# Local attention with a squared-Relu network behind it: in the last sequence, the scores of one and a half tiles in one stretch of the split TensorE array

## The chip, the cores and the metric

The kernel runs on one core of one Trainium2 chip. The metric is the device time of one execution in microseconds (us); lower is better. A core has TensorE (PE; its weight loads are shown as PEld), VectorE (DVE), ScalarE (ACT), GpSimd (POOL) and SyncE (SP), which work side by side and wait for each other by semaphores. Each takes its own instructions in the order in which the program gives them.

## The reference

Four sequences of 768 positions and 8 heads of 64. Each query sees the 96 latest positions and the first 8 positions of the sequence (the global keys), with a bias that falls with the distance; then a two-layer network with a squared Relu.

```python
scores = scale * np.matmul(q, k.transpose(0, 1, 3, 2))          # q, k, v: [4, 8, 768, 64]
keep = is_global | is_local                                      # pos < 8; 0 <= rel < 96
dist = np.where(is_global & ~is_local, float(n_local), np.abs(rel))
scores = np.where(keep, scores - slopes[:, None, None] * dist, -1e9)
a = softmax(scores)
x = np.matmul(a, v)                       # transposed and reshaped to [3072, 512]
g = np.maximum(x @ w_in, 0.0) ** 2        # w_in: [512, 2048]
out = g @ w_out                           # w_out: [2048, 512]
```

## The kernel before

**Tiles, blocks and steps.** The 3072 rows are 24 tiles `j` of 128 rows, six to a sequence, so tiles 18 to 23 are the last sequence. Two tiles make a block of the network, and a block is worked in 8 steps, each for 256 of the 2048 hidden columns: 12 blocks, steps 0 to 95. Step `n` has a first product (`s1`, L697: 8 matmuls of 128x256 into one PSUM bank `hT`), a Relu on ScalarE (`relu`, L718), a square on VectorE (`sq`, L730, out `hs`, 14 buffers) and a second product (`s2`, L767: 4 matmuls of 128x512 into the two banks `acc` of the block). `hr`, between Relu and square, has two buffers.

**Attention of a tile.** POOL loads `q`, `k` and `v` of the tile (L203), SyncE transposes queries and keys by DMA into `qkT` (L410; 12 buffers of it, SyncE's queue is in order). The scores (`sc`, L469) contract over 64 rows alone, so even and odd heads use the two halves of the array at the same time: a pair of matmuls, one in each half, each into its own bank. The first tile of a sequence has 8 such matmuls and two banks; every other tile looks at its own keys and at those of the tile to its left, in 16 matmuls and four banks (two groups `g` of four heads, each with two banks). One contiguous run of such matmuls is called a stretch. ScalarE takes the exponential of each bank (`exp`, L515), VectorE multiplies it with the exponential of the bias and mask (`mul`, L540), TensorE multiplies with the values (`pv`, L582, one bank for each of two halves of the heads), VectorE normalizes (`norm`, L609 and L610), and SyncE transposes the result by DMA into `xT` (L669), which the first product of the block needs.

**Global keys.** The global keys are the first 8 of a sequence. They are not kept apart: the mask leaves the first 8 columns of the left tile free for them. When the scores of tile `j` are done, `gk` (L556) overwrites the first 8 keys of tile `j` in `qkT` with the global ones, and the scores of tile `j+1` read them as those of its left tile. So the scores of `j+1` cannot come before the scores of `j` and the copy behind them. `gv` (L627) does the same for the values.

**Banks.** Two of the 8 PSUM banks are `acc`. The other six are one ring, `G`, in which transposes, scores, `hT` and `pv` take banks in the order in which the program opens them: a new bank waits for the users of the one six before it.

**Order.** The program's order is written by a planner, `Plan.run`, before anything is emitted. Every operation has its dependences, its cost on each engine, a key, and the ring it takes banks from; the planner goes through time, and picks the operation with the least sum of earliest start and 0.01 times its key. A result reaches another engine only after a lag. Keys make the first product run about four steps ahead of the second. For a tile the key comes from `base`, 8 times its block, less a lead (14 here), with 4 more for the second tile of a block. Besides, the scores of tile `j` may not come before the first product of step `4*j - 12`.

```python
            if n >= 0 and j >= NFIRST:
                o["deps"].append(s1_ops[n // NSTEP, n % NSTEP])
```

The kernel, as far as the diff touches it, with the line numbers of the profile:

Of the kernel before, what the change touches and what calls it, by code (L numbers as in the profile page):

```python
# [12 lines left out]
BF16 = mybir.dt.bfloat16  # L13
# [91 lines left out]
def kernel(  # L105
# [11 lines left out]
    nc = tc.nc  # L117
    B, H, S, D = q.shape
    P = 128
    d_model, d_ff = moe_w_in.shape  # L120
    assert D == 64 and S % 256 == 0 and H == 8 and d_model == H * D
    TPB = S // P
    NT = B * TPB
    NPAIR = H // 2
    KM = d_model // P
    KF = d_ff // P
    n_global = int(n_global)
# [8 lines left out]
    NSTEP = KF // 2  # L136
    NBLK = NT // 2
# [4 lines left out]
    NSPLIT = 4  # L142
    NBIAS = 3
    JQK, JX = 6, 8
    NQ, NKT = 3, 2 * TPB
# [9 lines left out]
    def const(shape, dt, name):  # L155
        return consts.tile(shape, dt, name=name, tag=name)
# [5 lines left out]
    qkT = [const([P, 2, NPAIR, P], BF16, f"qkT_{i}") for i in range(NKT)]  # L162
# [14 lines left out]
    plan = Plan()  # L177
    LEADS = {6: 10, 7: 11} | {j: 14 for j in range(10, NT)}
    SAFE = {j: 1.6 for j in range(6, 12)}
    SAFEX = {9: 1.5, 11: 1.5}  # L180
    JGATE = 11
    NHS = 14
    NWARM = 8
    NLATE, NO = 2, 4
    LEAD = 12
# [107 lines left out]
    for g in range(NFIRST + 2, NT, 6):  # L293
        js = range(g, min(g + 6, NT))
        o = plan.op(
            ("ones", g), {"DVE": 0.2}, lambda e, js=js: emit_ones(e, js),
            key=-1.0, ready=15.0,
        )
# [14 lines left out]
    def vec(cost):  # L313
        return {"DVE": cost}
# [20 lines left out]
    ]  # L335

    tiles = {}
    kT_users = [[] for _ in range(NKT)]
    qk_users = [[] for _ in qk_ring]
    xT_op = {}  # L340
# [5 lines left out]
    for j in range(NT):  # L346
        b, t = divmod(j, TPB)
        first = t == 0
        need = 8 * (j // 2)
        base = need - LEADS.get(j, LEAD) + 4 * (j % 2)  # L350


        if j in late:
# [3 lines left out]
            if NFIRST + 2 + NQ - 1 <= j < JGATE:  # L357

                def emit_gate(e, j=j):
# [4 lines left out]
                    key=base - 9,  # L364
# [3 lines left out]
                deps=qk_users[slot(j)] + [ones[j], gate], key=base, ready=issue[0],  # L368
# [7 lines left out]
        ku = kT_users[j % NKT]  # L376
        fp = j < NPLAIN
        parts = []
        for n in range(2) if j < JQK else ():
            users = []  # L380

            def emit_tr(e, j=j, n=n, fp=fp):
# [11 lines left out]
                deps=[land["qk"[n], j]], key=base, takes=(*G, [users]),  # L394
            )

            def emit_T(e, j=j, n=n, T_=T_):
                any_copy(e, T_[:, n], tiles.pop(("tr", n, j)))

            c = plan.op(  # L400
                ("T", n, j), {"DVE": 0.61 if fp else 0.41, "ACT": 0.48}, emit_T,
                deps=[tr] + ku, key=base + 0.1,
            )
# [4 lines left out]
        if j >= JQK:  # L408
            def emit_dT(e, j=j, T_=T_):
# [7 lines left out]
                deps=[land["q", j], land["k", j], xT_op[j - 3]] + ku, key=base - 6,  # L417
# [6 lines left out]
            parts = [T]  # L424
# [4 lines left out]
        groups = 1 if first else 2  # L429
# [32 lines left out]
                opened.add((odd, g))  # L462

        def emit_sc(e, gs, j=j, todo=todo, open_sc=open_sc):
            if j >= NBIAS:
                open_sc(gs)
            for g, pair, at, kt, odd in todo(gs):
                half = slice(odd * D, (odd + 1) * D)
                nc.tensor.matmul(  # L469
                    out=tiles["sc", j, odd, g][:, at, :],  # L470
                    lhsT=qkT[(j - kt) % NKT][half, 1, pair, :],
                    rhs=qkT[j % NKT][half, 0, pair, :],
                    start=j >= NBIAS,
                    stop=True,
                    skip_group_check=True,
                )

        deps = list(parts)
        if not first:
            deps += tiles["kready", j - 1] + [glob.get(("k", j - 1))]  # L480
        s_ = {}
        for gs in [(0,), (1,)] if j < NSPLIT and not first else [tuple(range(groups))]:
            n = 8 * len(gs)
            sc_users = busers[2 * gs[0] : 2 * gs[-1] + 2]
            takes = (*G, sc_users)
            bias = None
            if j < NBIAS:
                bias = plan.op(
                    ("bias", j, gs[0]), {"PE": 0.056 * n},
                    lambda e, gs=gs, f=emit_bias: f(e, gs), deps=[tr],  # L490
                    key=base + 0.9 + 2 * gs[0], takes=takes,
                )
                takes = None
            o = plan.op(
                ("sc", j, gs[0]), {"PE": 0.2 + 0.029 * n},
                lambda e, gs=gs, f=emit_sc: f(e, gs), deps=[*deps, bias],
                key=base + 1 + 2 * gs[0], takes=takes,
            )
            for us in sc_users:
                us.append(o)  # L500
            ku.append(o)
            if not first:
                kT_users[(j - 1) % NKT].append(o)
            s_.update({g: o for g in gs})
        for g in range(groups):
            for odd in range(2):
                users = busers[2 * g + odd]
# [41 lines left out]
                musers.append(m_)  # L549
                mul[odd, g], mul_users[odd, g] = m_, musers  # L550
        tiles["kready", j] = list(parts)


        if 1 <= t < TPB - 1:
            def emit_gk(e, j=j, t=t):
                nc.vector.tensor_copy(  # L556
                    qkT[j % NKT][:, 1, :, :n_global], qkT[(j - t) % NKT][:, 1, :, :n_global]
                )

            glob["k", j] = plan.op(  # L560
                ("gk", j), vec(0.1), emit_gk, deps=list(s_.values()), key=base + 4
            )
            kT_users[j % NKT].append(glob["k", j])
            kT_users[(j - t) % NKT].append(glob["k", j])
# [4 lines left out]
        for hf in range(2):  # L569
            users = []  # L570
# [167 lines left out]
    for o in plan.ops:  # L738
        if o["name"][0] == "sc":
            j = o["name"][1]  # L740
            n = 4 * j - LEAD
            if n >= 0 and j >= NFIRST:
                o["deps"].append(s1_ops[n // NSTEP, n % NSTEP])

    for blk in range(NBLK):
        last = blk == NBLK - 1
        acc_users = {}

        parts = [(0, None), (1, 0), (1, 1)] if last else [(0, None), (1, None)]
        order2 = (  # L750
            [(s, *p) for p in parts for s in range(NSTEP)]
            if last
            else [(s, *p) for s in range(NSTEP) for p in parts]
        )
        for s, sub, half in order2:
            users = acc_users.setdefault((sub, half), [])
            w = d_model if half is None else d_model // 2
            cols = slice(0, w) if half is None else slice(half * w, (half + 1) * w)
            own = half == 1

            def emit_s2(e, blk=blk, s=s, sub=sub, half=half, w=w, cols=cols, own=own):
                if s == 0:
                    pool, tag = (ps_g, "g") if own else (ps_acc, "acc")
                    tiles["acc", blk, sub, half] = pool.tile([P, w], FP32, name="acc", tag=tag)
                hs = tiles["hs", blk, s]
                for c in range(2):
                    nc.tensor.matmul(  # L767
                        out=tiles["acc", blk, sub, half],
                        lhsT=hs[:, c, sub * P : (sub + 1) * P],
                        rhs=w_out_sb[s][:, c, cols],  # L770
                        start=(s == 0 and c == 0),
                        stop=(s == NSTEP - 1 and c == 1),
                        skip_group_check=True,
                    )

            d, husers = square[blk, s]
            o = plan.op(
                ("s2", blk, s, sub), {"PE": 0.43 * w / d_model}, emit_s2,
                deps=[d, land["wout", s]] + users[-1:],
                key=8 * blk + s + 2.0 + (0 if not last else 8 * sub + 8 * (half or 0)),  # L780
                takes=((*G, [users]) if own else ("acc", NACC, [users])) if s == 0 else None,
            )
            users.append(o)
            husers.append(o)
            if s == NSTEP - 1:
                ousers = []

                def emit_o(e, blk=blk, sub=sub, half=half, cols=cols):
                    o_sb = work.tile([P, d_model], FP32, name="o", tag="o", bufs=NO)
                    any_copy(e, o_sb[:, cols], tiles["acc", blk, sub, half])  # L790
                    tiles["o", blk, sub, half] = o_sb

                ev = plan.op(
                    ("o", blk, sub), {"ACT": 0.48, "DVE": 0.61} if half is None else {"ACT": 0.28},
                    emit_o, deps=[o], key=8 * blk + s + 1.0, takes=("o", NO, [ousers]),
                )
                users.append(ev)
                ousers.append(ev)

                def emit_st(e, blk=blk, sub=sub, half=half, cols=cols):  # L800
                    r0 = (blk * 2 + sub) * P
                    nc.sync.dma_start(
                        out=out[r0 : r0 + P, cols],
                        in_=tiles.pop(("o", blk, sub, half))[:, cols],
                    )


                st = plan.op(
                    ("st", blk, sub), {"SP": 0.4}, emit_st,
                    deps=[ev, s1_ops[NLATE, 0] if blk < NLATE - 2 else None],  # L810
                    key=8 * blk + s + 9.0,
                )
                st = plan.op(("stored", blk, sub), {"DMAQ": 1.4}, None, deps=[st])
                ousers.append(st)
# [39 lines left out]
```

The softmax here doesn't subtract the row's maximum and nothing guards it: scores larger than these inputs give would overflow.

## Time and profile before

| | |
|---|---|
| time, median of 4 runs | 212.94 us (212.62 to 213.42) |
| the profiled execution | 212.88 us, of which its span 211.1 us |
| busy in the span | PE 203.5, PEld 142.3, DVE 142.2, ACT 117.6, POOL 73.9 us |
| granted clock of TensorE | 1.00 |
| first product, L697 | 768 matmuls, 98.3 us |
| second product, L767 | 369 matmuls recorded, 94.2 us |
| scores, L469 | 352 matmuls (192 of own keys, 160 of left keys) |
| in-place copies of global keys, L556 | 16 on VectorE, 215 ns each |

The span runs from the first to the last instruction, times in a timeline count from its start, and the rest of the execution's time lies around it. A line of a timeline gives start, length, engine, line of the kernel, operation, what it writes and reads, and how often; in brackets stands how long the engine was idle before, and for whom it waited. Matmuls are pipelined, so the lengths of neighbouring groups overlap, and the distance of their starts is the time that they take. Some matmul records are missing. The six stretches of the last sequence begin at 137.12, 144.74, 152.84, 160.93, 169.02 and 177.12 us.

### The profile page before, as it was taken

How to read it: one execution, taken by the hardware profiler on the slowest of the kernel's cores; microseconds unless marked ns; L12 is line 12 of the kernel's file. 1: busy time of each engine (PE TensorE's matmuls, PEld its weight loads, DVE VectorE, ACT ScalarE, POOL GpSimd, SP SyncE). 2: the span in 40 equal slices, each digit the busy share in tenths (PEclk: the TensorE clock that was granted, in tenths of full speed). 3: DMA queues.
4: the chain of work that ended last, by engine and by line, in shares of the span. 5: the costliest groups of instructions: out<-in, count | busy, mean ns of one | idle time of the engine just before them, and what ended most of it. 6: DMA issues, size and time to landing. Idle time of an engine off the chain costs nothing.

```text
span 211.1 us, 4968 instructions
## 1 busy us (share of the span) xinstructions
PE 203.5 (96%) x1953; PEld 142.3 (67%) x1984; DVE 142.2 (67%) x368; ACT 117.6 (56%) x221; POOL 73.9 (35%) x91
## 2 busy tenths in 40 slices
PE   7999999999999999999999999999999999999993
PEld 3777877656767766666676766666666766666772
DVE  7598878523877867876786786666786876644530
ACT  6797578114846755646456466456366465533531
POOL 8997765440675067140724505404000000000000
PEclk9999999999999999999999999999999999999999
DMA  8999999999999999959899997999443122120202
GB/s 124 154 170 187 183 191 199 176 215 130 178 146 151 174 135 168 224 70 153 85 199 143 137 198 97 138 171 133 86 106 75 45 82 28 25 99 3 99 0 101
DMA packets 112615, 27.32 MB, mean 129 GB/s; under 512 B 103248, under 2 KB 109648, under 8 KB 112592
## 3 DMA queue, kind: packets, MB, share of 16 engines
q0 software_dynamic: 79200, 13.37, 84.0%
q1 hardware_dynamic: 33392, 13.64, 32.2%
q8 instruction: 15, 0.25, 0.4%
q14 instruction: 8, 0.07, 0.1%
HBM read 27.26 MB, written 6.29 MB: 159 GB/s over the span
## 4 chain that ended last, share of the span: by engine, by line
PE 87%; POOL 5%; DMA 4%; issue 1%; ACT 1%; DVE 1%; POOLq 0%
PE hT L697 39%; PE acc L767 38%; PE sc L469 5%; PE po L582 4%; DMA win<-in_moe_w_in_dram 4%; POOL qk L203 3%; POOL v L203 2%; POOL win L203 1%; ACT hr L718 1%; PE tr L386 0%; PE trx L645 0%; DVE hs L730 0%; ACT esc L515 0%; ACT o L318 0%; DVE qkT L556 0%
## 5 line engine op out<-in xcount | busy, mean ns | idle before, releaser
L718 ACT ACTIVATE hr<-hT 128x512 f32<-128x512 f32 x96 | 58.1, 606 | 75.5 <-PE hT L697 73.3
L697 PE MATMUL hT<-xT,win 128*128 128x256 bf16 x768 | 98.3, 273 | 0.7 <-DMA win<-in_moe_w_in_dram 0.4
L767 PE MATMUL acc<-wout,hs 128*128 128x512 bf16 (+1 forms) x369 | 94.2, 370 | 2.0 <-issue 0.6
L697 PEld LDWEIGHTS <-win 128*128 128x128 bf16 x768 | 74.6, 98 | 26.7 <-DMA win<-in_moe_w_in_dram 0.7
L730 DVE TENSOR_TENSOR hs<-hr 128x512 bf16<-128x512 f32 x96 | 65.7, 688 | 34.2 <-ACT hr L718 33.9
L767 PEld LDWEIGHTS <-hs 128*128 128x128 bf16 x400 | 35.4, 98 | 22.1
L203 POOL DMA_DIRECT2D qk<-in_q_dram x23 | 20.8, 904 | 65.3 <-DMA qkT<-qk 49.6
L515 ACT ACTIVATE esc<-sc 128x512 bf16<-128x512 f32 x78 | 41.4, 612 | 1.2 <-PE sc L469 0.6
L540 DVE TENSOR_TENSOR at<-esc,E 128x512 bf16<-128x512 bf16 x78 | 31.9, 423 | 4.1 <-ACT esc L515 2.1
L203 POOL DMA_DIRECT2D v<-in_v_dram x24 | 21.9, 911 | 1.4 <-DMA win<-in_moe_w_in_dram 1.0
L610 DVE TENSOR_TENSOR x<-po,rs 128x256 bf16<-128x256 f32 x48 | 20.4, 425 | 1.7
L203 POOL DMA_DIRECT2D qk<-in_k_dram x23 | 20.7, 908 | 0.5 <-DMA win<-in_moe_w_in_dram 0.5
L582 PEld LDWEIGHTS <-at 128*128 128x128 bf16 x352 | 16.0, 98 | 6.2 <-issue 0.3
L582 PE MATMUL po<-v,at 128*128 128x65 bf16 x352 | 18.0, 193 | 0.3 <-DVE v L627 0.2
L318 ACT COPY o<-acc 128x512 f32<-128x512 f32 (+1 forms) x17 | 9.2, 563 | 8.1 <-PE acc L767 7.6
L469 PEld LDWEIGHTS <-qkT 64*128 64x128 bf16 x352 | 10.0, 94 | 5.5 <-issue 4.8
L469 PE MATMUL sc<-qkT 64*128 64x128 bf16 x192 | 13.2, 219 | 0.0
L609 DVE RECIPROCAL rs<-po 128x4 f32<-128x4 f32 x48 | 8.8, 184 | 6.1 <-PE po L582 5.4
L469 PE MATMUL sc<-qkT,qkT 64*128 64x128 bf16 x160 | 11.4, 216 | 0.0
L556 DVE COPY qkT<-qkT 128x32 bf16<-128x32 bf16 x16 | 3.4, 215 | 9.1 <-PE sc L469 9.0
L203 POOL DMA_DIRECT2D win<-in_moe_w_in_dram x8 | 6.2, 805 | 1.7 <-DMA win<-in_moe_w_in_dram 1.1
L320 DVE COPY o<-acc 128x512 f32<-128x512 f32 x8 | 5.5, 692 | 1.7 <-PE acc L767 1.6
(41 smaller groups left out, 64.6 us busy)
## 6 DMA issues: line engine op xcount, KB each, us to landing
out_dram<-o SPq DMA_DIRECT2D x23, 256.0 KB, 3.4
v<-in_v_dram POOLq DMA_DIRECT2D x24, 128.0 KB, 5.5
qk<-in_q_dram POOLq DMA_DIRECT2D x23, 128.0 KB, 5.0
qk<-in_k_dram POOLq DMA_DIRECT2D x23, 128.0 KB, 5.2
win<-in_moe_w_in_dram POOLq DMA_DIRECT2D x8, 256.0 KB, 8.0
wout<-in_moe_w_out_dram POOLq DMA_DIRECT2D x8, 256.0 KB, 9.2
qkT<-qk SPq DMA_TRANSPOSE x18, 5.4
plain<-in_q_dram SPq DMA_DIRECT2D x1, 256.0 KB, 3.3
```

The costliest lines, as they stand in the source:

```text
L203: nc.gpsimd.dma_start(out=dst, in_=src)
L318: nc.scalar.copy(dst, src)
L469: nc.tensor.matmul(out=tiles["sc", j, odd, g][:, at, :], lhsT=qkT[(j - kt) % NKT][half, 1, pair, :], rhs=qkT[j % NKT][half, 0, pair, :], s ...
L515: nc.scalar.activation(out=esc, in_=tiles.pop(("sc", j, odd, g)).rearrange("p a c -> p (a c)"), func=Act.Exp, scale=scale,)
L540: nc.vector.tensor_mul(at, tiles.pop(("esc", j, odd, g)), bias)
L582: nc.tensor.matmul(out=po[:, hi, :], lhsT=tiles["at", j, odd, g][:, at * P : (at + 1) * P], rhs=v_sb[kj][:, h, :], start=(i == 0), stop=(i ...
L609: nc.vector.reciprocal(rs, po[:, :, D : D + 1])
L610: nc.vector.tensor_tensor(out=x[:, 4 * hf : 4 * hf + 4, :], in0=po[:, :, :D], in1=rs.to_broadcast([P, 4, D]), op=Alu.mult,)
L697: nc.tensor.matmul(out=hT[:, c, :], lhsT=w_in_sb[s][:, kt, c * P : (c + 1) * P], rhs=tiles["xT", blk][:, kt, :], start=(kt == 0), stop=(kt ...
L718: nc.scalar.activation(hr, tiles.pop(("hT", blk, s)), Act.Relu)
L730: nc.vector.tensor_mul(hs, hr, hr)
L767: nc.tensor.matmul(out=tiles["acc", blk, sub, half], lhsT=hs[:, c, sub * P : (sub + 1) * P], rhs=w_out_sb[s][:, c, cols], start=(s == 0 an ...
```

## The change

The scores of tile 19 go into one operation, and so one stretch, with those of tile 18; the first half (group 0) of tile 21 with tile 20; tile 22 with the second half (group 1) of tile 21. Each of these takes all six banks of the ring. Tile 23 stays alone. The stretches are set right behind the first product of steps 60, 68, 74 and 80 (`STEP`), and the first product of the next step waits for them (`HOLD`). `base` of tiles 19, 21 and 22 is 4 less. So that the scores of 21 need not wait for the scores of 20, nor those of 22 for those of 21, the keys of tiles 20 and 21 are copied to a tile of their own (`kl`) when they have landed, with the global keys in the first 8 columns; the left-hand matmuls of 21 and 22 read them there, and `gk` of 20 and 21 is gone. `SETS` says for tiles 1 to 3 what the code said before; `BEHIND` is empty and does nothing.

```diff
+    SETS = {1: [(0,), (1,)], 2: [(0,), (1,)], 3: [(0,), (1,)], 21: [(0,), (1,)]}
+    JOIN = {(22, 0), (21, 0), (19, 0)}
+    COPY = [20, 21]
+    BEHIND = {}
+    HOLD = ((18, 0), (20, 0), (21, 1), (23, 0))
+    STEP = {(18, 0): 60, (20, 0): 68, (21, 1): 74, (23, 0): 80}
...
+    kl = [const([P, NPAIR, P], BF16, f"kl_{i}") for i in range(2 if COPY else 0)]
...
         base = need - LEADS.get(j, LEAD) + 4 * (j % 2)
+        if (j, 0) in JOIN:
+            base -= 4
...
         def emit_sc(e, gs, j=j, todo=todo, open_sc=open_sc):
+            if isinstance(gs, list):
+                for f, gs in gs:
+                    f(e, gs)
+                return
...
-                    lhsT=qkT[(j - kt) % NKT][half, 1, pair, :],
+                    lhsT=left[j - 1][half, pair, :] if kt else qkT[j % NKT][half, 1, pair, :],
...
-        for gs in [(0,), (1,)] if j < NSPLIT and not first else [tuple(range(groups))]:
+        for gs in SETS.get(j, [tuple(range(groups))]):
...
+            if (j, gs[0]) in JOIN:
+
+                o, also, taken = joint
+                also.append((emit_sc, gs))
+                taken += sc_users
+                o["deps"] += [d for d in deps if d is not None]
+                o["engines"]["PE"] += 0.029 * n
...
+        left[j] = qkT[j % NKT][:, 1]
+        if j in COPY:
+
+            left[j] = kl[COPY.index(j) % len(kl)]
+            users = left_users[j] = []
+
+            def emit_kl(e, j=j, t=t):
+                nc.vector.tensor_copy(left[j], qkT[j % NKT][:, 1])
+                nc.vector.tensor_copy(
+                    left[j][:, :, :n_global], qkT[(j - t) % NKT][:, 1, :, :n_global]
+                )
+
+            c = plan.op(
+                ("kl", j), vec(0.35), emit_kl, deps=parts, key=base - 3.5,
+                takes=("kl", len(kl), [users]),
+            )
...
-        if 1 <= t < TPB - 1:
+        if 1 <= t < TPB - 1 and j not in COPY:
             def emit_gk(e, j=j, t=t):
...
-            n = 4 * j - LEAD
+            n = STEP.get(o["name"][1:], 4 * j - LEAD)
             if n >= 0 and j >= NFIRST:
                 o["deps"].append(s1_ops[n // NSTEP, n % NSTEP])
+                if o["name"][1:] in HOLD:
+                    n += 1
+                    s1_ops[n // NSTEP, n % NSTEP]["deps"].append(o)
```

More of the change, by code (lines that the diff above doesn't have):

```diff
@@ L337 @@
     tiles = {}
+    left, left_users = {}, {}
+    kl = [const([P, NPAIR, P], BF16, f"kl_{i}") for i in range(2 if COPY else 0)]
     kT_users = [[] for _ in range(NKT)]
@@ L481 @@
         s_ = {}
-        for gs in [(0,), (1,)] if j < NSPLIT and not first else [tuple(range(groups))]:
+        for gs in SETS.get(j, [tuple(range(groups))]):
             n = 8 * len(gs)
             sc_users = busers[2 * gs[0] : 2 * gs[-1] + 2]
+            if (j, gs[0]) in JOIN:
[4 more added lines that the diff above has]
+                o["engines"]["PE"] += 0.029 * n
+                for us in sc_users:
+                    us.append(o)
+                ku.append(o)
+                if j - 1 in COPY:
+                    left_users[j - 1].append(o)
+                elif not first:
+                    kT_users[(j - 1) % NKT].append(o)
+                s_.update({g: o for g in gs})
+                continue
             takes = (*G, sc_users)
             bias = None
+            also = [(emit_sc, gs)]
             if j < NBIAS:
@@ L495 @@
                 ("sc", j, gs[0]), {"PE": 0.2 + 0.029 * n},
-                lambda e, gs=gs, f=emit_sc: f(e, gs), deps=[*deps, bias],
+                lambda e, gs=also, f=emit_sc: f(e, gs), deps=[*deps, bias],
                 key=base + 1 + 2 * gs[0], takes=takes,
             )
+            joint = o, also, sc_users
             for us in sc_users:
@@ L501 @@
             ku.append(o)
-            if not first:
+            if j - 1 in COPY:
+                left_users[j - 1].append(o)
+            elif not first:
                 kT_users[(j - 1) % NKT].append(o)
@@ L551 @@
         tiles["kready", j] = list(parts)
-        if 1 <= t < TPB - 1:
+        left[j] = qkT[j % NKT][:, 1]
[11 more added lines that the diff above has]
+            )
+            users.append(c)
+            kT_users[j % NKT].append(c)
+            kT_users[(j - t) % NKT].append(c)
+            tiles["kready", j] = [c]
+        if 1 <= t < TPB - 1 and j not in COPY:
             def emit_gk(e, j=j, t=t):
@@ L784 @@
             husers.append(o)
+            n = NSTEP * blk + s
+            m = n + max([d for at, d in BEHIND.items() if n >= at], default=0)
+            if m > n and m < NSTEP * NBLK:
+                o["deps"].append(s1_ops[m // NSTEP, m % NSTEP])
             if s == NSTEP - 1:
```

## The prediction

> **What bounds the kernel now.** I read the page first, its busy shares and its chain.
>
> ```profile
> PE 203.5 (96%) x1953; PEld 142.3 (67%) x1984; DVE 142.2 (67%) x368; ACT 117.6 (56%) x221; POOL 73.9 (35%) x91
> PE 87%; POOL 5%; DMA 4%; issue 1%; ACT 1%; DVE 1%; POOLq 0%
> L718 ACT ACTIVATE hr<-hT 128x512 f32<-128x512 f32 x96 | 58.1, 606 | 75.5 <-PE hT L697 73.3
> ```
>
> TensorE is busy for 96% of the span and carries 87% of the chain; ScalarE waits 73 us for it. The sequence that the change touches is the last, so I read the timeline of TensorE from 136 us on. Counting the groups of L697 (first product, 8 matmuls a step) back from the last, the one at 136.15 is step 60; counting the groups of L767 (second product, 4 a step) back, 137.44 is step 57.
>
> ```profile
> 136.15 1.04 PE L697 MATMUL hT<-xT,win 128*128 128x256 bf16 x8
> 137.12 0.40 PE L469 MATMUL sc<-qkT 64*128 64x128 bf16 x8
> 137.44 1.04 PE L767 MATMUL acc<-wout,hs 128*128 128x512 bf16 x4
> ...
> 142.04 1.04 PE L697 MATMUL hT<-xT,win 128*128 128x256 bf16 x8
> 142.91 1.03 PE L767 MATMUL acc<-wout,hs 128*128 128x512 bf16 x4
> 143.77 1.04 PE L697 MATMUL hT<-xT,win 128*128 128x256 bf16 x8
> 144.74 0.23 PE L469 MATMUL sc<-qkT 64*128 64x128 bf16 x2
> 144.81 0.22 PE L469 MATMUL sc<-qkT,qkT 64*128 64x128 bf16 x2
> ...
> 145.29 1.04 PE L767 MATMUL acc<-wout,hs 128*128 128x512 bf16 x4
> ```
>
> Read starts, not durations: a step of the first product followed by the second lasts 0.87 (142.04 to 142.91), a step of the second 0.86 (142.91 to 143.77). Nothing waits. Before the scores of tile 19 the same step lasts 0.97 (143.77 to 144.74), and the scores last 0.55 for 8 pairs of matmuls, whose starts are 0.056 apart (8 x 0.056 = 0.45). So going into the split array costs 0.10 and leaving it 0.10. Tile 18 says the same: 0.97 in, then 0.32 for 4 pairs (0.22 and 0.10). Of the 49.8 us from step 60 (136.15) to step 85 (185.98), 25 first-product steps (21.7), 25 second-product steps (21.6), the scores of tiles 18 to 23 (0.42 and five times 0.65) and eleven groups of attention-times-values (0.25 each) account for 49.7. TensorE has no idle time here to win back.
>
> Then what the other engines do with one stretch, from the full timeline:
>
> ```profile
> 137.22 0.60 ACT L718 ACTIVATE hr<-hT 128x512 f32<-128x512 f32 x1 [1.14 <-PE hT L697]
> ...
> 142.51 1.24 SPq L410 DMA_TRANSPOSE qkT<-qk  x1
> ...
> 145.34 2.06 ACT L515 ACTIVATE esc<-sc 128x512 bf16<-128x512 f32 x4
> 145.35 0.17 DVE L556 COPY qkT<-qkT 128x32 bf16<-128x32 bf16 x1 [0.92 <-PE sc L469]
> 145.47 0.69 DVE L730 TENSOR_TENSOR hs<-hr 128x512 bf16<-128x512 f32 x1
> ...
> 146.08 1.78 DVE L540 TENSOR_TENSOR at<-esc,E 128x512 bf16<-128x512 bf16 x4
> ```
>
> An exponential leaves a bank every 0.515 (2.06/4) and a bias multiplication every 0.445 (1.78/4). VectorE stood 0.92 behind the copy of the global keys.
>
> **What goes.** Six stretches of the split array become four: 18+19, 20 with half of 21, half of 21 with 22, and 23. The matmuls are the same in number and form, so what goes is two entries and two exits: 2 x (0.10 + 0.10) = 0.40 us, all on TensorE's own path.
>
> **What is added on VectorE.** Two copies of a tile's keys, 128x512 bf16 in SBUF, and two of its globals; the in-place global copies of tiles 20 and 21 go, and with them two waits of 0.92. The nearest row of a copy of this shape is the two of L326, 284 and 825 ns; I take 0.42, near the same shape from PSUM (L320, 421 ns). The global columns cost the 0.17 of L556 either way. So 0.6 to 1.6 us more work in all, 0.8 taken, beside TensorE: VectorE is busy for 10.9 of the 16 us from 137 to 153. It costs nothing while the copies run before the stretch at step 68 and in VectorE's idle time; ahead of a square that TensorE wants, one costs up to 0.8.
>
> **What is moved.** The scores of 19 come 4 steps earlier, of 22 two earlier, the second half of 21 two later. Each stretch is pinned behind one step (60, 68, 74, 80), and the next step waits for it. These waits are new on TensorE's queue: the sixth bank of a stretch is free only when the Relu of the step right before it is done (0.20 after that step ends plus 0.60, so 0.85), and the next step needs the first exponential's bank. Queued behind are that step and all after it. What covers the gap is the second product, which needs none of the six banks. At 137.02, where step 60 ends, steps 57, 58 and 59 of it are ready (the square of 59 ended at 136.80), 2.6 us. I place it so, t being the time after step 60 ends: one and a half steps (0 to 1.29), scores 18+19 (1.29 to 2.17: 12 pairs x 0.056 and 0.20), one and a half steps (to 3.46), then step 61. The first bank is done at about 1.62, its exponential runs about 1.82 to 2.42, so step 61 finds its bank a microsecond early. The gap costs 0.
>
> The burst behind it is six exponentials (3.1 us) where there were four. By the time step 62 of the second product is wanted, TensorE has done from 2.17 on: 2.15 of left second product, steps 61 to 64 (3.48), attention-times-values of 18 and 19 (0.75) and step 61 of the second product (0.86): t = 9.4. VectorE has by then to do from 2.3 on: six multiplications (2.67), four normalizations (0.18 and 0.42 and a little, 0.62 each, 2.48), one global copy (0.17) and two squares (1.38): 6.7, so t = 9.0. That is 0.4 us to spare where there were some 4 before. I take no stall; this is the thinnest cover.
>
> The Trainium skill speaks against the change here: TensorEngine Tiling (Array Packing), PSUM Bottleneck, says that tiling speeds up TensorE but not the emptying of PSUM, which may then bound. If TensorE stood through each burst of six, 3.1 us less 1.3 of second product, three stretches would cost some 5 us by that rule, an estimate. The row above decides otherwise: ACT is busy 56%.
>
> **Data for earlier stretches.** SyncE's queue is in order: the transposed load of tile 21 stands behind the transposed attention output of 18. In the profile it goes at 142.51; tile 18's scores start 1.3 later and its normalization meets a fuller VectorE, so I take 144.8. Its landing takes 3.1/5.4/8.6 (minimum, median, maximum of that group): 150.2, at worst 153.4; with the copy (0.42 and 0.17, at worst 0.825 and 0.17) 150.8 or 154.4. The stretch at step 68 wants it at about 153.8 (step 68 ends at 152.74, less 0.2 saved, and 1.3 of cover). So 3 us to spare, or 0.6 late. Tiles 19, 22 and 23 have more room. The attention output of 21 comes about 8 us after step 74 ends; step 80 is 11 us after it. POOL's loads are gated by older transposes, which do not move.
>
> **Sum.** Profiled run: 211.1 span and 1.78 around it, 212.88. 212.88 - 0.40 = 212.48; the median of the runs is 212.94, 0.06 above. I say 212.5, 0.2% less. A measurement of this kernel can tell some 0.3% (0.64 us) from no change: the four runs lie from 212.62 to 213.42.
>
> **Rivals.**
> - *Slower: VectorE falls behind after each six-bank burst, and TensorE waits for squares.* For it: 0.4 us to spare after 18+19, with exact pacing assumed; VectorE's waits of 0.2 to 0.9 in the timeline would eat that. Against: the later stretches have three normalizations, not four. Price: 0.9 of such waits less 0.4 is 0.5 a stretch, three times, less 0.40: +1.1, 214.0. It decides from 0.35 a stretch on (1.04/3).
> - *The key copy of tile 21 is late.* It needs a landing near the maximum; 0.6 once, less 0.40: 213.1.
> - *The gain is eaten exactly:* 0.1 to 0.2 a stretch: 212.9. The order is written for planned times, and small misfits add up.
> - *The joining does not happen:* if the planner put other matmuls between the halves there would be no gain. The code emits both lists in one operation, so I give this nothing.
> - *Faster by more than 0.3%:* nothing in the timeline has over 0.55 to give (0.40 and the 0.15 or so of remainder); only scatter of the runs would show it.
>
> **Chances.** Forecast (gapless, 212.5) 0.5, of which 0.2 may read as over 0.3% faster, being 0.24 us from that bound while the runs scatter by 0.4 either way; eaten exactly 0.14; late copy 0.06, half of it past the bound; VectorE behind 0.3. So faster 0.22, same 0.44, slower 0.34. The range reaches from the forecast less scatter (212.0) to the slower rival (214.0); the likeliest case's own is 212.0 to 212.9.
>
> **What would show it.** Right: four groups of L469 after 136 us, of 24, 24, 24 and 16 matmuls; about 0.97 for the step or half step ahead and 0.10 behind each; L767 on both sides of each with no idle time; L556 down from 16 to 14 copies; the last L767 ends 0.4 earlier. Wrong: idle time of PE at L767 released by the square (L730), or at L697 released by the exponential (L515), or at L469 released by a DVE copy; or the Relu (L718) waiting for VectorE in the 8 us after a stretch.

## The result, and the profile after

The changed kernel takes 212.59 us (median of 54 runs, 211.95 to 213.95), the kernel before 212.97 (78 runs): a ratio of 0.9981, 95% interval 0.9973 to 0.9989, or 0.40 us less by the ratio (0.38 between the medians). Its profiled execution took 212.33, with a span of 210.6. Runs over 1.5% longer than the fastest of the same kernel are in no median and no ratio below (none here, five of the twelve of x9_seq3_49, from 217.51 to 220.91, and one each of x8_seq3 and x11_seq3_50).

The page shows the same kernel as before in nearly every row: TensorE's busy time is half a microsecond less, VectorE's 0.4 more, and `gk` (now L612) has two copies fewer.

```profile
PE 203.0 (96%) x1954; PEld 142.2 (68%) x1984; DVE 142.6 (68%) x371; ACT 117.5 (56%) x220; POOL 73.9 (35%) x91
...
PE 87%; POOL 5%; DMA 4%; issue 1%; ACT 1%; DVE 1%; POOLq 0%
...
L612 DVE COPY qkT<-qkT 128x32 bf16<-128x32 bf16 x14 | 4.1, 294 | 6.8 <-PE sc L485 6.7
```

TensorE's timeline of the changed kernel from step 60 on. L753 is now the first product, L826 the second, L485 the scores, L638 attention times values:

```profile
136.04 1.04 PE L753 MATMUL hT<-xT,win 128*128 128x256 bf16 x8
136.91 1.46 PE L826 MATMUL acc<-wout,hs 128*128 128x512 bf16 x6
138.31 0.45 PE L485 MATMUL sc<-qkT 64*128 64x128 bf16 x10
138.59 0.22 PE L485 MATMUL sc<-qkT,qkT 64*128 64x128 bf16 x2
...
139.08 1.47 PE L826 MATMUL acc<-wout,hs 128*128 128x512 bf16 x6
140.39 1.91 PE L753 MATMUL hT<-xT,win 128*128 128x256 bf16 x16
142.13 0.65 PE L638 MATMUL po<-v,at 128*128 128x65 bf16 x16
...
153.81 0.23 PE L485 MATMUL sc<-qkT 64*128 64x128 bf16 x2
...
167.58 0.23 PE L485 MATMUL sc<-qkT 64*128 64x128 bf16 x2
...
177.02 0.23 PE L485 MATMUL sc<-qkT 64*128 64x128 bf16 x2
...
201.08 1.04 PE L753 MATMUL hT<-xT,win 128*128 128x256 bf16 x8
```

Six matmuls (one and a half steps) of the second product stand before the stretch of tiles 18 and 19, six behind it, and then step 61; no row there has an idle time. The six stretches of before are four. The whole result is in one distance: from the first matmul of step 60 to that of step 95 it is 65.04 us (136.04 to 201.08), and 65.47 before (136.15 to 201.62). The end of it before:

```profile
201.62 1.04 PE L697 MATMUL hT<-xT,win 128*128 128x256 bf16 x8
```

This distance is a sharper measure than the time. Up to step 40 TensorE's order is the same in all kernels of this study, and yet step 40 begins between 95.4 and 96.6 in the profiles: that much scatter comes from the part before, which the change does not touch.

### The profile page after: what moved, and what is told of

Read it like the earlier page. It is cut to its first block, busy times and chain, and to the rows that moved or that the text cites. A ratio compares the mean times of both kernels' runs of the same rounds, so it can differ in the third digit from the quotient of the medians.

```text
span 210.6 us, 4971 instructions
## 1 busy us (share of the span) xinstructions
PE 203.0 (96%) x1954; PEld 142.2 (68%) x1984; DVE 142.6 (68%) x371; ACT 117.5 (56%) x220; POOL 73.9 (35%) x91
## 4 chain that ended last, share of the span: by engine, by line
PE 87%; POOL 5%; DMA 4%; issue 1%; ACT 1%; DVE 1%; POOLq 0%
PE hT L753 39%; PE acc L826 38%; PE sc L485 5%; PE po L638 4%; DMA win<-in_moe_w_in_dram 4%; POOL qk L211 3%; POOL v L211 2%; POOL win L211 1%; ACT hr L774 1%; PE tr L398 0%; PE trx L701 0%; DVE hs L786 0%; ACT esc L551 0%; DVE qkT L612 0%; ACT o L326 0%
## 5 line engine op out<-in xcount | busy, mean ns | idle before, releaser
L753 PE MATMUL hT<-xT,win 128*128 128x256 bf16 x768 | 97.7, 273 | 0.7 <-ACT xT L326 0.4
L774 ACT ACTIVATE hr<-hT 128x512 f32<-128x512 f32 x96 | 58.0, 604 | 71.7 <-PE hT L753 63.6
L826 PE MATMUL acc<-wout,hs 128*128 128x512 bf16 (+1 forms) x370 | 93.0, 370 | 2.0 <-issue 0.6
L753 PEld LDWEIGHTS <-win 128*128 128x128 bf16 x768 | 74.2, 98 | 24.8 <-DMA win<-in_moe_w_in_dram 1.2
L786 DVE TENSOR_TENSOR hs<-hr 128x512 bf16<-128x512 f32 x96 | 65.4, 687 | 33.9 <-ACT hr L774 33.3
L826 PEld LDWEIGHTS <-hs 128*128 128x128 bf16 x400 | 36.0, 98 | 24.0
L638 PEld LDWEIGHTS <-at 128*128 128x128 bf16 x352 | 15.7, 98 | 5.6 <-ACT at L551 0.7
L638 PE MATMUL po<-v,at 128*128 128x65 bf16 x352 | 17.5, 193 | 0.5 <-ACT at L551 0.3
L485 PEld LDWEIGHTS <-qkT 64*128 64x128 bf16 x336 | 9.8, 94 | 5.8 <-issue 5.1
L485 PE MATMUL sc<-qkT 64*128 64x128 bf16 x192 | 12.9, 219 | 0.0
L485 PE MATMUL sc<-qkT,qkT 64*128 64x128 bf16 x144 | 10.3, 216 | 0.0
L612 DVE COPY qkT<-qkT 128x32 bf16<-128x32 bf16 x14 | 4.1, 294 | 6.8 <-PE sc L485 6.7
L328 DVE COPY o<-acc 128x512 f32<-128x512 f32 x9 | 6.2, 692 | 3.5 <-PE acc L826 3.4
```

The source lines that it names most:

```text
L485: nc.tensor.matmul(out=tiles["sc", j, odd, g][:, at, :], lhsT=left[j - 1][half, pair, :] if kt else qkT[j % NKT][half, 1, pair, :], rhs=qk ...
L638: nc.tensor.matmul(out=po[:, hi, :], lhsT=tiles["at", j, odd, g][:, at * P : (at + 1) * P], rhs=v_sb[kj][:, h, :], start=(i == 0), stop=(i ...
L753: nc.tensor.matmul(out=hT[:, c, :], lhsT=w_in_sb[s][:, kt, c * P : (c + 1) * P], rhs=tiles["xT", blk][:, kt, :], start=(kt == 0), stop=(kt ...
L774: nc.scalar.activation(hr, tiles.pop(("hT", blk, s)), Act.Relu)
L786: nc.vector.tensor_mul(hs, hr, hr)
L826: nc.tensor.matmul(out=tiles["acc", blk, sub, half], lhsT=hs[:, c, sub * P : (sub + 1) * P], rhs=w_out_sb[s][:, c, cols], start=(s == 0 an ...
```

## The experiments

Each was timed against the kernel before on the same chip; the ratio is to those runs. The distance is from step 60 to step 95 in its profile; the last column, from step 40 to step 60, matters where tiles 14 to 16 are joined.

| kernel | time, us | ratio to before (95%) | 60 to 95 | 40 to 60 |
|---|---|---|---|---|
| before | 212.97 | | 65.47 | 40.47 |
| changed | 212.59 | 0.9981 (0.9973 to 0.9989) | 65.04 | 40.47 |
| x1_full_between | 213.51 | 1.0017 (0.9998 to 1.0037) | 65.69 | |
| x2_full_before | 212.40 | 0.9963 (0.9936 to 0.9990) | 65.06 | |
| x3_one_join | 212.57 | 0.9980 (0.9962 to 0.9998) | 65.25 | |
| x4_copy_only | 212.76 | 1.0001 (0.9978 to 1.0024) | 65.47 | |
| x5_copy_4x | 213.61 | 1.0031 (1.0012 to 1.0050) | 66.25 | |
| x6_step67 | 215.25 | 1.0109 (1.0083 to 1.0135) | 67.19 | |
| x7_step67_early | 212.84 | 0.9995 (0.9976 to 1.0014) | 65.20 | |
| x8_seq3 | 214.06 | 1.0051 (1.0025 to 1.0077) | 65.72 | 41.01 |
| x9_seq3_49 | 214.40 | 1.0062 (1.0025 to 1.0099) | 70.95 | 40.26 |
| x10_room | 212.91 | 0.9995 (0.9966 to 1.0023) | 65.04 | 40.47 |
| x11_seq3_50 | 213.71 | 1.0027 (1.0001 to 1.0053) | 65.04 | 40.94 |
| x12_seq3_late_copy | 212.78 | 0.9998 (0.9976 to 1.0019) | 65.04 | 40.79 |

**Is it the entries and exits?** One tiny matmul over the whole array between the joined halves, and, as a control, ahead of them:

```diff
-                for f, gs in gs:
-                    f(e, gs)
+                for n_, (f, g_) in enumerate(gs):
+                    f(e, g_, full=len(gs) > 1 and n_ == 1)      # control: n_ == 0
...
+            if full:
+                nc.tensor.matmul(
+                    out=tiles["sc", j, 0, gs[0]][:, 0, :1], lhsT=ident, rhs=zero[:, :1],
+                    start=True, stop=True, skip_group_check=True,
+                )
```

> The changed kernel with one tiny matmul over the full array (128 rows, one output column) between the two halves of each of the three joined stretches, into a bank that the second half overwrites. Order and planner are those of the changed kernel. Theory (the gain is two exits and two entries of the split array, 0.10 us each): three more exits and entries, 3 x (0.20 + about 0.03) = 0.7 slower than the changed kernel, so 0.3 slower than before, 213.3 (ratio to before 1.0013). Rival (the gain comes from the new order or from VectorE's two waits that are gone): no slower than the changed kernel, 212.6.

> Control for the one between the halves: the same tiny matmul, but ahead of each joined stretch, where the array is whole already. Theory: its own time only, 3 x 0.03 = 0.1 over the changed kernel, 212.7 (ratio to before 0.9985). If the added instruction itself, and not the exit and entry, made the other one slow, this one is as slow.

TensorE's timeline with the matmul between the halves of 18 and 19:

```profile
139.28 0.40 PE L490 MATMUL sc<-qkT 64*128 64x128 bf16 x8
139.61 0.18 PE L484 MATMUL sc<-zero,ident 128*128 128x1 bf16 x1
139.72 0.23 PE L490 MATMUL sc<-qkT 64*128 64x128 bf16 x2
```

Four pairs would end at 139.50 (4 x 0.056); the matmul of one column starts at 139.61 and the next pair at 139.72, 0.22 for nothing but leaving and entering. Three of them make 65.69, 0.65 over the changed kernel; ahead of the stretch the same three cost 0.02. So an exit and an entry cost 0.21, and the instruction costs nearly nothing. In the times the two kernels are 0.5% apart.

**Does half of it give half?** Only 19 joined with 18; and only the copies, with nothing joined:

```diff
-    JOIN = {(22, 0), (21, 0), (19, 0)}
-    COPY = [20, 21]
+    JOIN = {(19, 0)}                                            # x4_copy_only: set()
+    COPY = []                                                   # x4_copy_only: [20, 21]
```

with `HOLD` and `STEP` for tile 18 alone, or for none, and tile 21 no longer split in `SETS`.

> Only tile 19 is joined with 18 (behind step 60, step 61 held); no key copies; tiles 20 to 23 as before. Five stretches. Theory: half the gain, 0.20, 212.8 (ratio 0.9991). Rival (the gain needs the key copies, that is VectorE's waits): no gain. Rival (six-bank bursts cost, and the gain is what is left of more): another amount than 0.20.

> The keys of tiles 20 and 21 are copied with the global ones, the in-place copies of these two tiles are gone, and nothing is joined, moved or held. Six stretches. Theory: no difference from before, 212.95 (ratio 1.000), since VectorE's waits and copies lie beside TensorE. Rival (VectorE's waits behind the in-place copies counted): up to 0.4 faster.

65.47, 65.25, 65.04 for none, one and two stretches fewer: the same 0.21 each time. The copies alone change the distance by nothing (65.47), so VectorE's waits behind the in-place copies of tiles 20 and 21, 0.92 each before, were beside the path. The medians cannot say this much; their intervals are as wide as the effect.

**How thick is VectorE's cover,** the time by which a square is there before TensorE wants it? In the changed kernel the copy of the keys of tile 20 (L595, L596) stands right ahead of the square of step 62; L774 is the Relu and L786 the square. From its full timeline:

```profile
145.24 0.60 ACT L774 ACTIVATE hr<-hT 128x512 f32<-128x512 f32 x1 [2.21 <-DVE rs L665]
...
145.52 1.04 POOL L211 DMA_DIRECT2D v<-in_v_dram  x1
145.60 0.28 DVE L683 COPY v<-v 8x520 bf16<-8x520 bf16 x1
145.80 0.27 DVE L595 COPY kl<-qkT 128x512 bf16<-128x512 bf16 x1
...
146.10 0.42 DVE L596 COPY kl<-qkT 128x32 bf16<-128x32 bf16 x1
...
146.19 2.70 DVE L786 TENSOR_TENSOR hs<-hr 128x512 bf16<-128x512 f32 x4
...
147.21 1.03 PE L826 MATMUL acc<-wout,hs 128*128 128x512 bf16 x4
```

The first of the four squares is that of step 62. With the 0.69 of one square it is done at 146.88, and 147.21 is where TensorE takes it: 0.33 to spare. I made the copy four times:

```diff
-                nc.vector.tensor_copy(left[j], qkT[j % NKT][:, 1])
+                for _ in range(4 if j == 20 else 1):
+                    nc.vector.tensor_copy(left[j], qkT[j % NKT][:, 1])
```

> The changed kernel with the 128x512 copy of the keys of tile 20 made four times in a row instead of once; the planner does not know of it. In the changed kernel's profile the copy took 0.27 and stands right ahead of the square of step 62, which is done at 146.88 and wanted at 147.21. Theory (that cover of 0.33 is what keeps VectorE off the path): three more copies, 0.8 to 0.9 us, make TensorE wait about 0.5 for the square of step 62, so 0.5 over the changed kernel, 213.1. Rival (VectorE has room, 67% busy, and the work is lost in its idle time): no change, 212.6.

```profile
146.48 1.75 DVE L596 COPY kl<-qkT 128x512 bf16<-128x512 bf16 x4
...
148.26 0.17 DVE L597 COPY kl<-qkT 128x32 bf16<-128x32 bf16 x1
148.35 2.70 DVE L787 TENSOR_TENSOR hs<-hr 128x512 bf16<-128x512 f32 x4
...
149.09 1.04 PE L827 MATMUL acc<-wout,hs 128*128 128x512 bf16 x4 [1.03 <-DVE hs L787]
```

TensorE waits 1.03 for exactly that square, and the distance grows by 1.21. The three copies took more than expected, 1.48 (1.75 less 0.27); less the 0.33 of cover that is 1.15, and TensorE starts 0.05 after the square ends (149.04 to 149.09): 1.20. (The idle time in brackets is smaller, 1.03, since it counts from the modelled end of the matmul before, 0.16 after the next could have started: a matmul of the second product is 0.38 long, and its neighbours start 0.22 apart. By starts, as I read the waits below, it is 1.20.) So the place and the cover were right; the price of a copy was not.

**What is the next limit?** The stretch of 20 and 21 one step earlier; and the same without the dependence that puts the transposed load of 21 behind the attention output of 18 on SyncE's queue (the last two lines):

```diff
-    STEP = {(18, 0): 60, (20, 0): 68, (21, 1): 74, (23, 0): 80}
+    STEP = {(18, 0): 60, (20, 0): 67, (21, 1): 74, (23, 0): 80}
...
-                deps=[land["q", j], land["k", j], xT_op[j - 3]] + ku, key=base - 6,
+                deps=[land["q", j], land["k", j], xT_op[j - 3] if j != 21 else None] + ku, key=base - 6,
```

> The changed kernel with the stretch of tiles 20 and 21 behind step 67 instead of 68. In the changed kernel's profile the transposed load of tile 21 was issued at 145.90, behind the transposed attention output of 18, and landed at 154.15; the first matmul that reads it came at 154.27. Theory (this load is the next limit): the stretch wants it at about 152.3, so TensorE waits up to 2 us in the middle of it: 1 to 2 over the changed kernel, 213.6 to 214.6; less if the load lands sooner than in that run. Rival (the load is not close): 212.6.

> As the kernel with the stretch behind step 67, and the planner need no longer put the transposed load of tile 21 behind the attention output of 18 on SyncE's queue. Theory: the load goes some 6 us sooner, right behind that of tile 20, and TensorE does not wait: 212.6, as the changed kernel. If the kernel with step 67 is slow for another reason (banks, VectorE), this one is as slow.

The first is 2.1 slower than the changed kernel in the distance, but not by the wait that I expected. The planner too seems to take the load to come late: it did not place the stretch behind step 67, and steps from 69 on, which are not held, went ahead and took the banks:

```profile
155.98 7.15 PE L753 MATMUL hT<-xT,win 128*128 128x256 bf16 x64
163.06 0.23 PE L485 MATMUL sc<-qkT 64*128 64x128 bf16 x2
...
165.80 0.35 PE L638 MATMUL po<-v,at 128*128 128x65 bf16 x6 [0.40 <-DVE at L576]
167.27 0.81 PE L826 MATMUL acc<-wout,hs 128*128 128x512 bf16 x3 [1.12 <-DVE rs L665]
```

Eight steps of the first product in a row, the stretch ten microseconds late, and then TensorE waits for VectorE. With the load freed of its place in the queue the stretch begins at 152.35 and the distance is 65.20. The remaining 0.16 is a wait for the square of step 62 again: the copy of the global values ahead of it (L683) took 0.71 there, 0.28 in the changed kernel, and that alone uses up the cover. So the load of 21 and its place on SyncE, as the planner reckons them, set how early this stretch can come. The wait itself was not run; but in x6 the copy that waits for the load started at 153.66, and in x7's stretch the weights of tile 21 are loaded from 152.76 on, so some 0.9 would have been missing.

**Room alone.** The changed kernel with that load sooner, and with three buffers for the attention output `x` instead of two:

> The changed kernel with room alone: the third buffer for x and the transposed load of tile 21 sooner; stretches as in the changed kernel. Theory (TensorE waits for neither in the changed kernel): no change, 212.6, steps 60 to 95 in 65.04. Rival (in some executions it does wait for the load of tile 21, which had 0.12 to spare in the profile): up to 0.3 faster in the median.

65.04, as the changed kernel: in the two profiled executions TensorE waits for neither. The time cannot be told from that of before or of the changed kernel (0.9966 to 1.0023).

**The same in the sequence before.** Tiles 14 to 16 joined in the same manner should give 0.21 more:

```diff
-    JOIN = {(22, 0), (21, 0), (19, 0)}
-    COPY = [20, 21]
-    STEP = {(18, 0): 60, (20, 0): 68, (21, 1): 74, (23, 0): 80}
+    JOIN = {(22, 0), (21, 0), (19, 0), (16, 0), (15, 0)}
+    COPY = [14, 15, 20, 21]
+    STEP = {(14, 0): 45, (15, 1): 50, (17, 0): 56, (18, 0): 60, (20, 0): 68, (21, 1): 74, (23, 0): 80}
```

and `SETS` and `HOLD` to match. The later three all have `x` with three buffers and the load of 21 sooner; x9 and x12 have 49 for 50 besides, and x12 the loads of 20 and 21 planned 4 us later by `SAFE`, so that the copies stand later on VectorE.

> The changed kernel, and in the sequence before the last the same for tiles 14 to 17: tile 14 with half of 15 behind step 45, the other half with 16 behind step 50, 17 behind step 56, each with the next step held; keys of 14 and 15 copied too. One stretch fewer than in the changed kernel, seven joined ones' places counted (12, 13, 14+15, 15+16, 17 there). Theory: 0.21 less than the changed kernel, 212.4 (ratio to before 0.997), if the transposed loads of 15 and 16 are there in time. Rival (that part of the kernel is bound by its loads): a wait of TensorE at the scores, no gain or up to 2 slower.

> As the kernel with tiles 14 to 16 joined, a third buffer for x and the sooner load of tile 21, but with the second joined stretch behind step 50 as at first. Theory: the wait of a normalization for a transposed read is gone (about 0.6), the wait of step 56 for the attention output of 15 stays (0.6): between the first such kernel and the one with step 49, 213.0 to 213.4.

> As the kernel that joins tiles 14 to 16 too, with three changes for what made TensorE wait there: the second joined stretch behind step 49 instead of 50, so that the attention output of 15 is transposed sooner; a third buffer for the attention output x, so that a normalization need not wait for a transposed read; and the transposed load of tile 21 no longer behind the attention output of 18. Seven stretches before it from tile 14 on become... five joined or single ones are saved down to one fewer than in the changed kernel. Theory (one more stretch gone is 0.21, if the data are there): 212.4, ratio to before 0.997, steps 40 to 95 in 105.3 us (changed kernel 105.51). Rival (loads still bind that sequence): 0.3 to 1.5 slower than the changed kernel, with TensorE waiting for a transposed DMA.

> As the kernel with tiles 14 to 16 joined behind step 49, but the planner takes the transposed loads of tiles 20 and 21 to land 4 us later, so that the two key copies stand two squares later in VectorE's queue (there VectorE stood 3.9 at the first of them and TensorE 4.1 behind its squares). Theory (one more stretch gone is 0.21 wherever the data are there, and the copy's place in VectorE's queue made the loss): steps 40 to 60 in 40.26 as there, steps 60 to 95 in 65.04 as in the changed kernel, 212.4, ratio to before 0.997. Rival (the loads that moved with the earlier stretches are late whatever the copy's place): TensorE waits again behind step 60, 213 or more.

None beats the changed kernel. Behind step 50 (x8, x11), step 56 waits for the transposed attention output of 15, in x8 0.58 by the bracket, in x11:

```profile
128.70 1.05 PE L753 MATMUL hT<-xT,win 128*128 128x256 bf16 x8 [0.51 <-DMA xT<-x]
```

By starts it is 0.74 and 0.67; less the 0.21 gained, that makes the 41.01 and 40.94. x8 lost another 0.7 behind step 60, where a normalization waited 1.00 for the transposed read of `x` that had not left its buffer; with the third buffer (and the sooner load of 21) in x11 that is gone, 65.04. Behind step 49 (x9) the 0.21 is there, 40.26 against 40.47, but the key copies of tile 20 and 21 now stand at a place in VectorE's queue where the load has not landed. From the timeline of x9:

```profile
148.44 0.29 DVE L595 COPY kl<-qkT 128x512 bf16<-128x512 bf16 x1 [3.88 <-DMA qkT<-qk]
...
150.74 4.12 DVE L786 TENSOR_TENSOR hs<-hr 128x512 bf16<-128x512 f32 x6
...
151.47 4.24 PE L826 MATMUL acc<-wout,hs 128*128 128x512 bf16 x12 [4.05 <-DVE hs L786]
```

VectorE stands 3.88 at a copy that nobody needs yet, and six squares stand behind it; TensorE waits 4.05 in one piece, 4.22 by starts. That is not all of the 5.91 by which the distance is longer: behind the wait the twelve matmuls take 4.03 (151.47 to 155.50), where twelve at the usual distance take 2.59 (12 x 0.216), and the granted clock in the profile is 0.50 from 153.0 to 156.0, and 1.00 up to 151.4 and from 156.0 on. The slower matmuls make the other 1.7. (This execution took 218.29; the kernel's twelve lie from 213.33 to 220.91. With one profile kept, it is not shown how much of that is the landing.) With the copies planned later (x12) the distance behind step 60 is 65.04 again and the runs lie closer, from 211.65 to 214.37; but between 40 and 60 it is 40.79, and that is the same fault at the first of the key copies of tiles 14 and 15:

```profile
101.94 0.29 DVE L595 COPY kl<-qkT 128x512 bf16<-128x512 bf16 x1 [0.70 <-DMA qkT<-qk]
...
104.05 0.59 PE L826 MATMUL acc<-wout,hs 128*128 128x512 bf16 x2 [0.38 <-DVE o L328]
```

VectorE waited 0.70 for the load, its copy out of `acc` (L328) behind it ended at 104.00, and TensorE, which needed that bank, stood 0.54 by starts: all of the difference to the 40.26 of x9. So the 0.21 is there when no copy waits; whether an order gets it in most executions stays open.

## Why the prediction was right

**The sum** was the entries and exits, 0.40, and nothing else. Measured: 0.43 in the distance, 0.40 by the ratio of the times, 0.21 for each exit and entry by itself. Forecast 212.5, measured 212.59. The change is real but smaller than the 0.3% that I said one measurement can tell; it took some fifty runs, or the distance in the profile.

**The placing around the first stretch** came out to hundredths: scores 1.40 after step 60 ends (138.31 - 136.91; predicted 1.29 and the entry), the first exponential at 1.83 (predicted 1.82), step 61 at 3.48 (predicted 3.46). The second product does cover the emptying of all six banks, so the rule on PSUM's emptying did not bind; no row of TensorE in the last 70 us has an idle time over 0.16, and the two that have it stand where a matmul record is missing. The prediction set that rule aside by ScalarE's busy share of 56%, a mean of the whole span; what decided was the second product that was ready on both sides of the stretch.

**The thin cover at step 62** was predicted 0.4, and is 0.33; but both sides of it were short, and the errors cancel. I had VectorE done at t = 9.0 and TensorE there at 9.4. Measured it is 9.97 and 10.30. VectorE's sum left out the copy of the global values (L683) and the copies for tile 20, which fell just there and took 0.59 by starts (145.60 to 146.19), and a wait of 0.71 for the first attention-times-values; its normalizations were shorter, 0.55 and not 0.62. TensorE's sum left out step 65 of the first product, which goes ahead. The rival that hangs on this cover was not far off: x5 brings it about with 1.5 us of VectorE's work.

**The key copy** was taken at 0.42 and took 0.27 and 0.29, near the lower of the two rows of its shape. The copy of the globals was taken at 0.17 "either way" and took 0.42 once, but the square behind it starts 0.09 later all the same (146.10 to 146.19).

**The data of tile 21** is the step that failed. I gave the load 3 us to spare by its median landing. It was issued at 145.90 (predicted 144.8) and landed 8.2 later, near the longest of its group, and the copy that waited for it started at 154.17; the first pair of matmuls of tile 21 in that stretch comes at 154.27, and its weights are loaded one pair ahead, at 154.21. So less than 0.1 to spare, and not 3. The rival also named the wrong reader: the copy of 21 is read by the next stretch, and here the transposed queries and keys themselves are wanted. In this execution its price was not paid, by luck rather than by cover.

```profile
145.90 1.24 SPq L422 DMA_TRANSPOSE qkT<-qk  x1
...
154.17 0.29 DVE L595 COPY kl<-qkT 128x512 bf16<-128x512 bf16 x1 [0.23 <-DMA qkT<-qk]
...
154.27 0.22 PE L485 MATMUL sc<-qkT 64*128 64x128 bf16 x2
```

**The step behind which the third stretch stands** was read as 74. `HOLD` keeps back step 75 alone: step 76, which has no such dependence, goes before the stretch, and 75 after it. It cost nothing here; in x6 the same thing, with step 68 held and 69 free, cost 2.1.

## What to carry to other kernels

Where TensorE is gapless, what can be won is what lies between its instructions: count the entries into and exits from the split array, and price them by the distance of starts on both sides. What a longer stretch takes from its neighbours (banks, VectorE's order, the landing of loads) is paid only when the cover is gone, and a cover must be reckoned with the longest landing that the profile has seen, not the median. (Even that is no bound: the longest of these loads took 8.6 in the profile before, 8.4 in the changed kernel's and 9.9 in that of x6.) A copy placed early in an in-order queue is no gift: it holds up all behind it until its data are there.

## What the runs showed of the hardware that I had not expected

The key copy of 128x512 took 0.27 to 0.31 in most places and 0.51 to 0.65 in others, and the copy of 128x32 took 0.17 to 0.18 or 0.42 to 0.62; in x5 four equal copies in a row took 0.28, 0.54, 0.29 and 0.54. All 14 long ones in the profiles here overlap a DMA issue of POOL in time (145.52 for 1.04 in the rows above, beside the copy of 0.42), and the short one at 154.50 (0.18) came after POOL's last issue. But 20 of the short ones overlap one too, the copy of 0.27 at 145.80 with its whole length. The Trainium skill, Advanced Engine Details and Errata, VectorE Performance Modes, says that VectorE's second port is shared with GpSimd and that the two hinder each other in the two-port modes; that would fit the first finding, and does not by itself explain the second. No run here isolates it.
